# Reordering the queues of the first steps in a fused linear-attention and SoLU kernel

## The chip, the cores and the metric

The kernel runs on one core of a Trainium2 chip. The metric is the device time of one launch in microseconds (us), the median of five runs. A profile is one further execution, recorded by the hardware profiler.

## What is computed

Two blocks follow each other. The first is a recurrence over 768 positions for 4 batches x 8 heads with a 40 x 40 state each:

```
for t in range(S):
    y[t]  = rt @ state
    Sa    = state @ at
    state = state * wt - outer(Sa, bt) + outer(vt, kt)
```

The second takes y, 3072 tokens of 320 numbers, through a feed-forward block:

```
h  = x @ w_in                      # 320 -> 1024
sm = exp(h - max(h)) / (sum + 1e-9)
s  = h * sm
ln = (s - mean(s)) / sqrt(var(s) + 1e-6) * g_ln
out = ln @ w_out                   # 1024 -> 320
```

All inputs are float32 except w_in and w_out, which arrive as float64 and have to be narrowed on the chip.

## The kernel before

The recurrence is done in chunks of 64 positions. A step i treats two of the four batches of one chunk, so there are 24 steps (N); a round n is a chunk with both of its steps, 12 rounds. A step passes through several generators, each of which yields where another's work may be put between:

- `front` (from line 383) with `decay` (L345 to L374): decay factors by exponentials, the scaled k, b and a, transposes of a and b (L400, L289), and the triangular matrix nt of the chunk (pnt, L308, masked by VectorE in L311).
- `scatter` and `gather` (L424, L434, L439): the diagonal blocks of nt go to DRAM and come back with one block per partition (blk). For rounds 0 to 3 the blocks are 16 wide (`FINE`).
- `invert` or `invert_fine` (from L441): VectorE inverts the blocks column by column, a multiply and a subtract each (L456, L458). In rounds 0 to 3 one call sets up, fourteen do a column each, and a last one copies u on ScalarE (L462) and stores it by two transfers on SP (L464).
- `bring_inverse` (L499): four transfers on SP's queue bring the inverted blocks u into tinvT. Round 0 needs them for its second step only.
- `solve`: from the blocks to the inverse of the whole 64 x 64 matrix. Its first yield for i > 0 is VectorE's transposition of tinvT (L598); then py, y (L602), pz and so on (L547 for every product). For i = 0 it builds the inverse on TensorE by doubling (L584 to L593).
- `attend`: transposes of k, v and r (L289; prT is r's), the masked scores psi and lamv, and the product px.
- `recurrence` and `readout`: carry the state across chunks (px at L663, x at L665, pu at L684, nuT, lamu, sm), and give y (pyo, L723; x at L730).
- `repack` (L741 to L744, twelve transfers on SP), `hidden`, `output`: the feed-forward block, six steps (`LAG`) behind the recurrence. `store` (L812) writes a round's output by two transfers on SP.
- `weights`: fetches the 26 float64 pieces of w_in and w_out on POOL's queue (L228) and narrows them: VectorE (L179, L181), ScalarE (L184, L185), VectorE (L187, L189, L191); two calls per piece.

The order of everything is written by hand. `turns(order, ...)` reads a string; each letter advances one generator by a yield, and `I` by as many as a list of counts says. The letters: r recurrence, y readout, a attend of the next step, s solve of the next step, f and g the fronts of the step or steps five ahead, I the inverse, W the weights, B `arrivals`, X `repacked`, L a later load of b and k, * filler matmuls. Every engine and every DMA queue works its instructions off in that order.

A prologue prepares rounds 0 and 1 before step 0. Step 0 uses the second string of `EARLY` (it has two fronts), steps 1 to 5 the first. In odd steps `arrivals` brings the inverted blocks of round (i + 1) / 2 and gathers those of the round after. Step 0 ends with the scatter of round 2 and then with loads of round 3's k and round 1's r, two transfers each (L335), all on SP. A load of an input is two transfers of 64 x 16 rows of 160 bytes.

Of the kernel before, what the change touches and what calls it, by code (L numbers as in the profile page):

```python
# [19 lines left out]
L = 64  # L20
AHEAD = 5
LAG = 6
# [34 lines left out]
def doubling_masks():  # L57

    s, t = np.arange(P)[:, None] % L, np.arange(L)[None, :]
    return np.concatenate([(s // (2 * b) == t // (2 * b)) & (s & b == 0) & (t & b != 0) for b in (1, 2, 4, 8)],  # L60
                          1).astype(np.float32)
# [3 lines left out]
def kernel(  # L65
# [28 lines left out]
    nc = tc.nc  # L94
    B, H, S, D = r.shape
# [3 lines left out]
    NCH = S // L  # L99
# [176 lines left out]
    def half(p):  # L276
        return slice(64 * p, 64 * p + 64)
# [41 lines left out]
    of_round = [dict() for _ in range(NCH)]  # L319

    def load(n, *names, by=(nc.sync, nc.sync)):

        if n >= NCH:
            return
        d = of_round[n]
        for name in names:
            ap = dict(w=w, b=b, a=a, k=k, v=v, r=r)[name]
            if name in "vr":
                d[name] = dict(v=v_t, r=r_t)[name][n % 2]
                to = d[name].rearrange("q s h c -> q (s h) c")[:, :, 0:D]  # L330
            else:
                d[name] = raw.tile([P, 2, H, D], FP32, tag="raw_" + name, name="raw_" + name)
                to = d[name].rearrange("q s h c -> q (s h) c")
            for c in range(2):
                by[c].dma_start(out=to[half(c)], in_=ap[2 * c:2 * c + 2, :, n * L:(n + 1) * L, :]  # L335
                                  .rearrange("b h t d -> t (b h) d"))
# [39 lines left out]
    def quarter(q):  # L376
        return slice(Q * q, Q * q + Q)

    def homes(q, steps=slice(0, 2)):

        return slice((q * 2 + steps.start) * H, (q * 2 + steps.stop) * H)
# [36 lines left out]
    def scatter(n):  # L418

        d = of_round[n]  # L420
        d["blocks"] = dram.tile([64, Q, Q], FP32, tag="blk_dram", name="blk_dram")
        nt = d["nt"].rearrange("q s p g t -> q (s p g) t")
        for q in range(4):
            nc.sync.dma_start(out=d["blocks"][homes(q)].rearrange("h s t -> s h t"),  # L424
                              in_=nt[quarter(q), :, quarter(q % 2)])

    def gather(n):


        if n < FINE:  # L430
            R = Q // 2
            nb = of_round[n]["nb"] = two.tile([P, R, R], FP32, tag="blk", name="blk", bufs=2)
            for z in range(2):
                nc.sync.dma_start(out=nb[half(z)],  # L434
                                  in_=of_round[n]["blocks"][:, R * z:R * z + R, R * z:R * z + R])
            return
        nb = of_round[n]["nb"] = two.tile([P, Q, Q], FP32, tag="blk", name="blk", bufs=2)
        for p in range(2):
            nc.sync.dma_start(out=nb[half(p)], in_=of_round[n]["blocks"])  # L439
# [55 lines left out]
    def bring_inverse(n, steps=slice(0, 2)):  # L495

        u = of_round[n]["u"]
        for q in range(4):
            nc.sync.dma_start(  # L499
                out=ti_t[quarter(q), steps, :, :, quarter(q % 2)].rearrange("s z p g t -> s (z p g) t"),  # L500
                in_=u[homes(q, steps)].rearrange("h s t -> s h t"))
# [307 lines left out]
    def store(n):  # L809
        rows = out.rearrange("(b s) d -> s b d", b=B)[n * L:(n + 1) * L]  # L810
        for c in range(2):
            nc.sync.dma_start(out=rows[:, 2 * c:2 * c + 2, :], in_=of_round[n]["osb"][half(c)])  # L812

    def steps(part, n):
        for _ in range(n):
            if part:
                next(part, None)

    def turns(order, more, **parts):

        for x in order.split():
            n = more.get(x, 1)
            steps(parts.get(x), n.pop(0) if isinstance(n, list) else n)

    def fronts(i):

        return [j for j in ((4, 5) if i == 0 else (i + AHEAD,)) if j < N]

    EARLY = ("r r a r B W f I r r W I W s y r X W a I s f L W a I a s W f I a f W s I a f W s f W",
             "r r a r W f r r W g W s y r W a f g L W a I a s f g W a I s f g W I s a f g W I s f g W I")  # L830
    STEADY = "r b r a r B f b b o r o I o r o s y o r X I o h a f L a s a h f a I h f s h f h a f h"
    CENTRE = "r r a r f o I r o r o s y o r X I o h a f L a s a h I f s a h I f s h f s h I a f h"
    LATE = "r b r r a B b b r o o I o r o s y o r X I o h a L a s a h a I h s h h a h"
# [9 lines left out]
    def inverses():  # L843
        for n in range(1, NCH):
            yield from invert(n)

    def inverse_steps(i):

        if i == 0:
            return [5, 5, 5, 1, 0]  # L850
        if i == LAG - 1:
            return [0, 0, 4, 4, 3, 3]
        if i == LAG:
            return [3, 3, 4, 4, 4]
        if i < LAG:
            return [0, 0, 2, 2, 2, 2] if i % 2 else [3, 3, 1, 1, 0, 0]
        return [0, 7, 7] if i % 2 else [6, 7, 5]

    def warm(n, x):

        for _ in range(n):
            nc.tensor.matmul(idle[:, 0:x.shape[1]], lhsT=x[:, 0:P], rhs=x, start=True, stop=True)

    def fillers():
        while True:
            warm(1, sm_t[0].rearrange("q c g d -> q (c g d)")[:, 0:256])
            yield
# [5 lines left out]
    def arrivals(i):  # L873

        n = (i + 1) // 2
        if n < NCH:
            bring_inverse(n)
        if n + 1 < NCH:
            gather(n + 1)
        yield  # L880

    def later(n, *names):
# [3 lines left out]
    with tc.manual_schedule():  # L886
        both = (nc.sync, nc.scalar)
        load(0, "w", "b", "a", by=both)
        nc.scalar.dma_start(out=masks, in_=nc.inline_tensor(doubling_masks(), name="masks").ap())
        load(0, "k", "v")  # L890
        load(1, "w", "a", "b")
        warm(3, sm_t[0].rearrange("q c g d -> q (c g d)"))
        f, g, at, inv, so, ws = front(0), front(1), attend(0), invert(0), solve(0), weights()
        turns("f g f g f f g g f f f g g s g a", {}, f=f, g=g, s=so, a=at)
        f, g, warmer = front(2), front(3), fillers()
        scatter(0)
        load(0, "r")
        gather(0)
        load(1, "k")
        load(2, "w")  # L900
        turns("f g s f s * g a s f I s I f a s I g I s I g a I", dict(I=[2, 3, 3, 3, 3, 99]), f=f, g=g, s=so, a=at, I=inv,
              **{"*": warmer})
        load(2, "a", "b")
        bring_inverse(0, slice(1, 2))
        turns("s f W s * f a s a g s g f g W W", {}, f=f, g=g, s=so, a=at, W=ws, **{"*": warmer})
        scatter(1)
        load(2, "k")
        gather(1)
        load(1, "v")
        begin(0)  # L910
        inv = inverses()
        after, before = None, None
        for i in range(N):
            m, more, js = i - LAG, i + 1 < N, fronts(i)
            now = hidden(m) if m >= 0 else None
            parts = dict(r=recurrence(i), y=readout(i), I=inv, W=ws, h=now, b=after, o=before)
            if i == LAG:
                steps(ws, 99)
                parts["o"] = centre()
                steps(parts["o"], 1)  # L920
            parts.update(zip("fg", (front_of[j] for j in js)))
            if more:
                parts.update(a=attend(i + 1), s=solve(i + 1))
            if i % 2 == 0:
                load((i + 6) // 2, "w", "a")
                parts["L"] = later((i + 6) // 2, *("bk" if i else "b"))
            else:
                parts["X"] = repacked(i // 2)
                parts["B"] = arrivals(i)
            order = EARLY[len(js) - 1] if i < LAG else CENTRE if i == LAG else STEADY if js else LATE  # L930
            turns(order, dict(I=inverse_steps(i)), **parts)
            if i % 2:
                load((i + 3) // 2, "v", "r")
            if js and js[-1] % 2:
                scatter(js[-1] // 2)
            if i == 0:
                load(3, "k")
                load(1, "r")
            begin(i + 1)
            after, before = now, output(m) if m >= 0 else None  # L940
        for m in range(N - LAG, N):
            now = hidden(m)
            turns("b h h h h h o o h b b o o o o", {}, h=now, b=after, o=before)
            after, before = now, output(m)
        turns("b b b o o o o o o", {}, b=after, o=before)
# [30 lines left out]
```

## Time and profile before

| what | value |
|---|---|
| median of 5 runs | 677.42 us |
| the five runs | 676.04, 676.88, 677.42, 678.99, 685.69 us |
| profiled execution, its own time | 671.89 us |
| its span, first to last instruction | 669.8 us |
| mean granted TensorE clock | 0.973 |
| busy: PE, VectorE, ScalarE, POOL | 609.8, 443.2, 275.8, 119.2 us |
| pu of steps 1, 2, 3, 4, 5 on TensorE starts at | 72.69, 100.64, 121.32, 141.49, 164.12 us |

In the views, PE is TensorE and PEld its weight loads, DVE is VectorE, ACT ScalarE, POOL GpSimd, and SPq the issuing of transfers on SyncE's queue. A line of a timeline has start and length in us, engine, source line, operation, the tile written and those read, shapes, and how many instructions are merged (x4). What stands in square brackets is the idle time of the engine just before and what ended it. The time of an SPq line is that of issuing, not of the transfer.

### The profile page before, as it was taken

How to read it: one execution, taken by the hardware profiler on the slowest of the kernel's cores; microseconds unless marked ns; L12 is line 12 of the kernel's file. 1: busy time of each engine (PE TensorE's matmuls, PEld its weight loads, DVE VectorE, ACT ScalarE, POOL GpSimd, SP SyncE). 2: the span in 40 equal slices, each digit the busy share in tenths (PEclk: the TensorE clock that was granted, in tenths of full speed). 3: DMA queues.
4: the chain of work that ended last, by engine and by line, in shares of the span. 5: the costliest groups of instructions: out<-in, count | busy, mean ns of one | idle time of the engine just before them, and what ended most of it. 6: DMA issues, size and time to landing. Idle time of an engine off the chain costs nothing.

```text
span 669.8 us, 28595 instructions
## 1 busy us (share of the span) xinstructions
PE 609.8 (91%) x12579; PEld 430.4 (64%) x12579; DVE 443.2 (66%) x1203; ACT 275.8 (41%) x663; POOL 119.2 (18%) x219
## 2 busy tenths in 40 slices
PE   7787677888789999999999999999999999999996
PEld 4566566766666677667667667676765666555554
DVE  4459477584896786886876876976967844333423
ACT  3264554566335344534534443452443334412312
POOL 4424312331121121122112112211200100000000
PEclk9897779998899999999999999999999999999999
DMA  9769748485362545454453543554234020000000
GB/s 156 110 150 153 131 82 151 85 138 105 85 104 48 98 87 95 72 94 89 80 94 82 88 88 75 83 102 89 38 74 72 24 43 18 22 24 21 20 21 20
DMA packets 238155, 53.74 MB, mean 80 GB/s; under 512 B 227400, under 2 KB 235344, under 8 KB 238032
## 3 DMA queue, kind: packets, MB, share of 16 engines
q1 hardware_dynamic: 232928, 45.80, 40.1%
q0 software_dynamic: 1696, 5.25, 3.1%
q8 instruction: 99, 1.62, 1.1%
q10 hardware_dynamic: 3408, 0.87, 0.9%
q14 instruction: 24, 0.20, 0.1%
HBM read 36.95 MB, written 10.22 MB: 70 GB/s over the span
## 4 chain that ended last, share of the span: by engine, by line
PE 65%; DVE 14%; ACT 7%; issue 5%; DMA 4%; SPq 3%; ACTq 1%; DVEq 0%
PE po L799 16%; PE h L754 13%; PE pyo L723 4%; PE pz L547 3%; PE pcx L370 3%; PE plnT L794 3%; PE py L547 3%; DVE prod L486 3%; DVE u L488 2%; PE pcum L357 2%; PE plamv L308 2%; DMA raw_w<-in_w_dram 2%; DVE nmax L764 2%; PE ppsi L308 2%; PE plamu L308 2%
## 5 line engine op out<-in xcount | busy, mean ns | idle before, releaser
L754 PE MATMUL h<-w_in,xT 128*128 128x512 f32 (+1 forms) x288 | 125.0, 624 | 0.0
L799 PE MATMUL po<-w,lnT 128*128 128x320 f32 x384 | 115.9, 440 | 3.2 <-ACT lnT L795 3.2
L799 PEld LDWEIGHTS po<-w,lnT 128*128 128x128 f32 x384 | 68.3, 190 | 29.2 <-ACT lnT L795 5.8
L488 DVE TENSOR_TENSOR u<-u,prod 128x30 f32<-128x30 f32 (+7 forms) x240 | 66.6, 278 | 8.2
L486 DVE TENSOR_TENSOR prod<-blk,u 128x30 f32<-128x30 f32 (+7 forms) x240 | 65.9, 274 | 7.0
L764 DVE TENSOR_REDUCE nmax<-h 128x1 f32<-128x1024 f32 x24 | 29.3, 1222 | 52.4 <-PE h L754 52.4
L360 POOL TENSOR_TENSOR kx<-raw_b,inv 128x320 f32<-128x320 f32 x24 | 21.1, 877 | 233.5 <-ACT inv L358 214.3
L754 PEld LDWEIGHTS h<-w_in,xT 128*128 128x128 f32 (+1 forms) x288 | 38.0, 188 | 29.7 <-issue 27.7
L804 ACT ACTIVATE osb<-po,rs 128x320 f32<-128x320 f32 x24 | 12.7, 528 | 98.9 <-PE po L799 87.3
L795 ACT COPY lnT<-plnT 128x512 f32<-128x512 f32 x48 | 27.0, 587 | 41.5 <-PE plnT L794 41.4
L786 POOL TENSOR_TENSOR rs<-c,mhalf 128x1 f32<-128x1 f32 x24 | 13.2, 550 | 151.7 <-DVE c L785 150.6
L311 DVE TENSOR_TENSOR lamv<-plamv,cst 128x512 f32<-128x512 f32 x24 | 16.6, 690 | 29.9 <-PE plamv L308 29.0
L771 DVE TENSOR_TENSOR e<-h,e 128x1024 f32<-128x1024 f32 x24 | 29.4, 1224 | 10.1 <-ACT e L768 9.6
L768 ACT ACTIVATE e<-h,nmax 128x1024 f32<-128x1024 f32 x24 | 26.8, 1116 | 20.7 <-DVE nmax L764 15.3
L547 PE MATMUL py<-tinv,nt 32*32 32x32 f32 x1280 | 24.0, 196 | 12.3 <-DVE tinv L598 10.7
L633 ACT ACTIVATE tinvT<-pz 32x256 f32<-32x256 f32 x48 | 17.9, 374 | 41.0 <-PE pz L547 40.6
L370 PE MATMUL pcx<-cst,lw 128*128 128x132 f32 x192 | 32.2, 293 | 2.8 <-DVE y L602 1.5
L370 PEld LDWEIGHTS pcx<-cst,lw 128*128 128x128 f32 x192 | 26.7, 194 | 11.2 <-ACT y_mid L629 3.5
L372 ACT ACTIVATE kx<-pcx 128x264 f32<-128x264 f32 x48 | 18.9, 393 | 32.8 <-PE pcx L370 32.5
L709 POOL TENSOR_TENSOR sm<-tot,fac 128x320 f32<-128x320 f32 x20 | 14.8, 741 | 97.8 <-DVE tot L708 65.9
L776 DVE BATCH_NORM_STATS2 bs<-e 128x6 f32<-128x512 f32 x48 | 30.8, 684 | 0.6
L547 PEld LDWEIGHTS py<-tinv,nt 32*32 32x32 f32 x1280 | 20.2, 110 | 16.9 <-issue 12.7
(139 smaller groups left out, 1174.9 us busy)
## 6 DMA issues: line engine op xcount, KB each, us to landing
blk<-blk_dram SPq DMA_DIRECT2D x16, 256.0 KB
raw_k<-in_k_dram SPq DMA_DIRECT2D x24, 160.0 KB
v<-in_v_dram SPq DMA_DIRECT2D x24, 160.0 KB
r<-in_r_dram SPq DMA_DIRECT2D x24, 160.0 KB
out_dram<-osb SPq DMA_DIRECT2D x24, 160.0 KB
raw_w<-in_w_dram SPq DMA_DIRECT2D x23, 160.0 KB
raw_b<-in_b_dram SPq DMA_DIRECT2D x23, 160.0 KB
raw_a<-in_a_dram SPq DMA_DIRECT2D x23, 160.0 KB
```

Of the source, the lines that this page charges most:

```text
L308: nc.tensor.matmul(t[half(c ^ p * cross), p, g * L:(g + 1) * L], lhsT=lhs[half(p), g, half(c)], rhs=rhs[half(p), g, half(c)], start=True, ...
L370: nc.tensor.matmul(t[:, g * 132:g * 132 + 132], lhsT=pair(lw, 2 * j + g), rhs=cst[:, lo:lo + 132], start=True, stop=True)
L486: nc.vector.tensor_tensor(out=t, in0=nb[:, j:j + 1, j + 1:Q].to_broadcast([P, rows, m]), in1=u[:, 0:rows, j:j + 1].to_broadcast([P, rows, ...
L488: nc.vector.tensor_tensor(out=u[:, 0:rows, j + 1:Q], in0=u[:, 0:rows, j + 1:Q], in1=t, op=ALU.subtract)
L547: nc.tensor.matmul(t[quarter(out), c:c + Q], lhsT=lhs(p, g), rhs=rhs(p, g), start=True, stop=True)
L754: nc.tensor.matmul(h[:, j * 512:j * 512 + 512], lhsT=of_round[i // 2]["xT"][rows, kt, i % 2 * P:i % 2 * P + P], rhs=w_in[rows, 4 if kt == ...
L764: nc.vector.tensor_reduce(out=nmax, in_=h, axis=AX.X, op=ALU.max, negate=True)
L768: nc.scalar.activation(out=e, in_=h, func=AF.Exp, bias=nmax, accum_out=esum)
L771: nc.vector.tensor_tensor(out=q, in0=h, in1=e, op=ALU.mult)
L776: nc.vector.bn_stats(out=bs[:, j], in_=q[:, j * 512:j * 512 + 512])
L795: nc.scalar.copy(out=lnT[:, fs.start:fs.stop].rearrange("p f t -> p (f t)"), in_=t)
L799: nc.tensor.matmul(o[:, 0:DM], lhsT=lnT[:, f, :], rhs=w2[:, f, :], start=f == 0, stop=f == NF - 1)
```

## The change

Four things are changed, all of them orders:

- In the prologue, VectorE's inverse of round 0 is called one solve step later at its beginning and at its end. One `s` moves from the second string of turns to the first. In step 0 the first call of the inverse moves behind `a s`, with 4 yields instead of 5, and the second does 6 instead of 5.
- The loads of round 3's k and round 1's r move from the end of step 0 into `arrivals` of step 1: k between the bringing of round 1's inverted blocks and the gather of round 2, r behind that gather.
- Steps 1 to 5 no longer share a string: odd ones call the weights 11 times instead of 9, even ones 7 times.
- The second transfer of the last round's output is issued on ScalarE's queue.

```
-            nc.sync.dma_start(out=rows[:, 2 * c:2 * c + 2, :], in_=of_round[n]["osb"][half(c)])
+            (nc.scalar if c and n == NCH - 1 else nc.sync).dma_start(out=rows[:, 2 * c:2 * c + 2, :], in_=of_round[n]["osb"][half(c)])
...
-    EARLY = ("r r a r B W f I r r W I W s y r X W a I s f L W a I a s W f I a f W s I a f W s f W",
-             "r r a r W f r r W g W s y r W a f g L W a I a s f g W a I s f g W I s a f g W I s f g W I")
+    EARLY = ("r r a r B W f I r r W I W s y r X W a I s f W a W I a s W f I a W f W s I a f W s f W",
+             "r r a r W f r r W g W s y r W a f g L W a a s I f g W a I s f g W I s a f g W I s f g W I",
+             "r r a r f I r r W I W s y r X W a I s f L W a I a s f I a f W s I a f W s f W")
...
         if i == 0:
-            return [5, 5, 5, 1, 0]
+            return [4, 6, 5, 1, 0]
...
             bring_inverse(n)
+        if i == 1:
+            load(3, "k")
         if n + 1 < NCH:
             gather(n + 1)
+        if i == 1:
+            load(1, "r")
...
-        turns("f g s f s * g a s f I s I f a s I g I s I g a I", dict(I=[2, 3, 3, 3, 3, 99]), f=f, g=g, s=so, a=at, I=inv,
+        turns("f g s f s * g a s f s I f a s I g I s I I g a s I", dict(I=[2, 3, 3, 3, 3, 99]), f=f, g=g, s=so, a=at, I=inv,
...
-        turns("s f W s * f a s a g s g f g W W", {}, f=f, g=g, s=so, a=at, W=ws, **{"*": warmer})
+        turns("f W s * f a s a g s g f g W W", {}, f=f, g=g, s=so, a=at, W=ws, **{"*": warmer})
...
-            order = EARLY[len(js) - 1] if i < LAG else CENTRE if i == LAG else STEADY if js else LATE
+            order = EARLY[1 if i == 0 else 0 if i % 2 else 2] if i < LAG else CENTRE if i == LAG else STEADY if js else LATE
...
-            if i == 0:
-                load(3, "k")
-                load(1, "r")
```

## The prediction, made before the result was known

> **What bounds the kernel now.** I read the page first, in the order of its parts. From step 6 on TensorE is the bound and nothing in the change touches that stretch except the last store; the slices before it are the only ones that leave room.
>
> ```profile
> PE 609.8 (91%) x12579; PEld 430.4 (64%) x12579; DVE 443.2 (66%) x1203; ACT 275.8 (41%) x663; POOL 119.2 (18%) x219
> PE   7787677888789999999999999999999999999996
> PEclk9897779998899999999999999999999999999999
> ```
>
> A slice is 16.7 us. PE shows 6 to 8 tenths up to slice 11 (about 200 us) and 9 afterwards, so time saved before 200 us is kept, because what follows is a full TensorE queue. Then the stretches of 2 us around the emptiest place, with PE, PEld, DVE, ACT, POOL, clock, DMA share and GB/s:
>
> ```profile
> 78.00:80.00 2.00, 0.53 (x4) 0.29 (x4) 0.42 (x1) 0.59 (x1) 1.74 (x4) 1.00 0.98 182
> 80.00:82.00 2.00, 0.00 (x0) 0.00 (x0) 0.00 (x0) 0.00 (x0) 1.72 (x4) 0.61 1.19 202
> 82.00:84.00 2.00, 0.00 (x0) 0.00 (x0) 0.00 (x0) 0.00 (x0) 0.00 (x0) 0.50 1.19 161
> 84.00:86.00 2.00, 0.00 (x0) 0.00 (x0) 0.39 (x1) 0.00 (x0) 0.00 (x0) 0.50 0.50 51
> ```
>
> Every engine stands still for 6 us while the DMA engines are full, and the granted clock falls to half. The timeline of SP's queue, VectorE and TensorE says for what:
>
> ```profile
> 70.55 1.13 SPq L464 DMA_DIRECT2D u_dram<-u  x2
> 72.50 2.01 SPq L424 DMA_DIRECT2D blk_dram<-nt  x4
> 74.55 1.37 SPq L335 DMA_DIRECT2D raw_k<-in_k_dram  x2
> 75.97 1.53 SPq L335 DMA_DIRECT2D r<-in_r_dram  x2
> 78.02 4.92 SPq L499 DMA_DIRECT2D tinvT<-u_dram  x4
> 82.98 1.90 SPq L434 DMA_DIRECT2D blk<-blk_dram  x2
> ...
> 85.61 0.71 DVE L598 STREAM_TRANSPOSE tinv<-tinvT 128x512 f32<-128x512 f32 x1 [7.19 <-DMA tinvT<-u_dram]
> ...
> 86.47 1.08 PE L547 MATMUL py<-tinv,nt 32*32 32x32 f32 x64 [7.94 <-DVE tinv L598]
> ...
> 89.72 1.11 PE L289 MATMUL prT<-cst,r 128*128 128x128 f32 x4
> ```
>
> The inverted blocks of round 1 (tinvT) stand in SP's queue behind two transfers of k and two of r. VectorE waits 7.19 us for them, TensorE 7.94 us for VectorE. The last line is the one to keep in mind: 3.25 us after the wait, TensorE needs that same r.
>
> **The change, part by part.**
>
> *Prologue: VectorE's inverse of round 0 behind the solve.* No instruction is added; VectorE's order changes. (On POOL the moved steps own two zeroings of u, 0.70 us at 57.10 in step 0, and pass nothing there.) Before, three columns of the inverse (28.26 to 29.56, 1.30 us) ran in a hole in which VectorE waited for psi (30.26, idle 0.70 before it). Now two other steps (0.71 us) run there, the 1.30 us fall behind psi, and the last column (0.39 us, 36.77 to 37.16) goes behind the solve's y (37.08). So y comes 1.30 - 0.39 = 0.9 us later, and TensorE's pz at 37.47, which waited 1.20 us for y, with it. The moved step also issues two copies on ScalarE (0.83 us at 37.20) and two u transfers on SP, ahead of loads of a and b; u comes about 1.3 us later, and nobody waited for it (its transpose at 52.25 shows no idle time). Bounds: 0 if a later wait absorbs it, 1.3 if the shorter queue gains nothing. I take 0.9 us later.
>
> *Step 0: four columns behind an eviction.* VectorE ran five inverse steps (57.71 to 59.70, 2.0 us) before y at 59.70, and TensorE's pz started at 60.15 after 1.70 us of idle. With y first it is ready near 58.0, and TensorE's 1.70 us go. The number of inverse steps stays 15 up to the third call, so the last column ends at 68.26 plus the 0.9 above, near 69.2. ScalarE's copies of u (70.09, behind two bT copies that follow TensorE and now come 1.7 - 0.9 = 0.8 us earlier) can start near 69.2 to 69.3: u's store moves from 70.55 to about 69.65, the scatter from 72.50 to 71.6. Bounds for this: 0 (VectorE alone decides) to 1.7 us; taken 0.9.
>
> *SP's queue in step 1.* Four tinvT issues pass four load issues (k, k, r, r), and the two gather issues pass r. tinvT can be issued when the scatter ends, 71.6 + 2.01, so 73.7 instead of 78.02. Where nothing stood in front (123.45 to 125.40 in a later step) four such issues took 1.95 us and the last landed at 127.18, 3.7 us after the first issue. So tinvT lands at 77.4 instead of 85.48: 8.1 us earlier, and if that were all, the step would follow.
>
> But now r is last. Its transfers are issued behind tinvT, k and the gather. Best case by the shortest rows: 1.95 + 1.37 + 1.35 (gather at 125.56) + 1.53 = 6.2 us after 73.7, so 79.9, and 1.8 us more to land: 81.7. Worst case: the same ten issues took from 74.55 to 84.88 before, 10.3 us, so 84.0, and 3.3 us more (82.14 to 85.48): 87.3. I take 86.0, near the worst, because the DMA share stood at 0.98 to 1.19 from 76 to 84: the engines were full, and the order does not shorten what they carry (weights on POOL's queue, 78.26 to 80.24, included). TensorE then reaches prT near 81 and stands until 86.1 instead of 89.72. Gain 3.6 us; ends 2.4 (89.72 - 87.3) and 8.0 (89.72 - 81.7). Behind prT queue pz, plamv and all the rest of step 1. VectorE, in order, first waits for the gathered blocks (before: 87.61), which now land before r. The output blocks (xT at 86.93) find SP free at about 84 and lose nothing.
>
> *The clock.* In the rows above an idle TensorE fell to 0.50, and kept it to 90.7. At 0.50 the 32-matmul groups take 1.06 to 1.13 us, at full clock 0.69. A wait of some 5 us at prT again ends at half clock; before, only 1 us of the work after prT fell into it. Four such groups more cost 4 x 0.4 = 1.6 us, of which VectorE, ahead by what it did in the wait, leaves perhaps 1.0. Ends 0 and 1.6; taken 1.0 us.
>
> [...]
>
> *Narrowing of the weights.* Odd early steps get 11 calls instead of 9, even ones 7. Two calls narrow one piece: on VectorE 0.29 + 0.29 + 0.42 + 0.42 + 0.43 = 1.85 us in step 1 (256 wide), 0.23 + 0.23 + 0.32 + 0.32 + 0.33 = 1.43 us in later ones (160 wide), plus two ScalarE evictions and POOL's fetch. In step 1 the wait for r covers it. Step 3 has VectorE idle only 0.95, 1.11, 0.18 and 1.05 us, at waits that stay; there up to 1.4 us can show. In step 5 the weights run out, as before. Steps 2 and 4 lose a piece each, where VectorE already waited up to 1.98, 2.46, 3.92 and 3.23 us for TensorE, so little comes back. Ends: 4.7 us lost (1.85 + 1.43 + 1.43) and 2.9 gained (two pieces); taken 0.4 us lost, nearest to step 3's rows less something from step 2.
>
> *The last store.* Its two issues took 1.25 us one after the other at 665.17; ScalarE's queue issues the second beside the first. Gain 0 to 0.63, taken 0.5 us.
>
> **Sum**: -3.6 + 1.0 + 0.4 - 0.5 = -2.7 us (the first two parts are inside the 73.7). The profiled execution took 671.89 us (span 669.8 and 2.1 around it) and would take 669.2. It lies 5.5 us under the median of the runs, 677.42, which I take to stay so: 677.4 - 2.7 = 674.7 us.
>
> **The rivals.**
> - *r is no obstacle.* It lands near 82, TensorE waits about 1 us and keeps its clock: -8.0 - 0.5 + 0.4 = -8.1, so 669.3 us. For it: the short issue times at 123 us. Against: the DMA shares over 0.98.
> - *The wait only changes its name.* r lands at 87.3 and the half clock takes 1.6: -2.4 + 1.6 + 0.4 - 0.5 = -0.9, or even nothing: 676.5 us. For it: the same ten transfers, the same full engines.
> - *Slower: the narrowing shows in the odd steps.* VectorE becomes the bound there and nothing comes back in even steps: 4.7 instead of 0.4 us, so -2.7 + 4.3 = +1.6, 679.0 us. It decides once more than 3.1 us of the 4.7 show. For it: step 3 leaves VectorE 3.3 us idle at waits that the new work doesn't fill. Against: the wait for r covers step 1.
>
> **How the numbers follow.** Forecast 0.50, r no obstacle 0.15, name only 0.23, slower 0.12. Predicted: 674.7. Four of the five runs lie between 676.04 and 678.99 (the fifth at 685.69), so each case has 1.5 to 2 us about it. 8 in 10 reach from the first rival to the third: 668.5 to 679.5. One per cent is 6.8 us, about what a measurement of this kernel can tell from no change. Faster by over that (under 670.6) needs most of the first rival and a little of the forecast's tail: 0.14. Slower by over it (above 684.2) has only the tail of the third: 0.04. Within: 0.82.
>
> **What the profile will show.** Right: tinvT issued by about 74 and VectorE's transposition near 78 without 7 us of idle; in its place a TensorE wait at prT for r of some 5 us, and prT near 86; no gap before the pz at 58; pz of the prologue 0.9 us later. Wrong: prT starting before 83 with no wait (first rival), or at 88 or later (second); or VectorE gaining more than 1 us per odd step ahead of TensorE's px, with pu waiting for x (third). The prediction fails outright if u's store is later than 70.55, since then nothing in step 1 moves forward.

## The result, and the profile after

The changed kernel takes 677.57 us (median of 46 runs), the kernel before 677.38 us (86 runs). The ratio is 1.0016, 95% interval [1.0000, 1.0031]: no gain, and at most 0.3% lost. The forecast had 2.7 us gained (674.7 us); the measured time is inside its range, and inside the case "within 1%", but the forecast gain did not come. The nearest of the four cases is "the wait only changes its name" (676.5 us).

The profiled execution of the changed kernel took 677.02 us (span 675.2, mean clock 0.964), close to its median. That of the kernel before took 671.89 us, 5.5 us under its median, so the two pages can't be subtracted. Most of their difference is probably the clock: up to 210 us the records of before show 34.1 us at half clock, those of after 44.4 us. As an estimate, 10.2 us at half clock cost at most half of that, 5.1 us, if TensorE worked through all of them; the spans differ by 5.4 us. All else is therefore compared inside one trace, from one event of a step to the next.

The busy row of TensorE and the row of its granted clock, 40 slices of 16.9 us, from the page of the changed kernel:

```profile
PE   6787677897798999999999999999999999999996
PEclk9879869799999999999999999999999899999999
```

The low stretch is as long as before: 6 to 9 tenths in the first 13 slices (before, 6 to 8 in the first 12), and 9 behind them. The stretches of 2 us around the place that the change aims at (busy PE, PEld, DVE, ACT, POOL, clock, DMA share, GB/s):

```profile
80.00:82.00 2.00, 0.00 (x0) 0.00 (x0) 0.00 (x0) 0.45 (x1) 1.95 (x5) 1.00 0.85 202
82.00:84.00 2.00, 0.00 (x0) 0.00 (x0) 0.00 (x0) 0.00 (x0) 0.13 (x1) 0.87 1.11 210
84.00:86.00 2.00, 0.83 (x62) 0.86 (x64) 1.69 (x4) 0.00 (x0) 0.00 (x0) 0.50 1.02 108
88.00:90.00 2.00, 0.48 (x20) 0.29 (x12) 1.97 (x7) 0.55 (x2) 0.58 (x1) 0.50 0.71 94
```

The hole is split in two. TensorE stands still from 79.8 to 85.2 us instead of from 78.5 to 86.5, and again before 90.7; the DMA engines are nearly as full as before, and the clock is at half from 83.5 on. The timeline of SP's queue, VectorE and TensorE at the same place:

```profile
72.98 1.13 SPq L464 DMA_DIRECT2D u_dram<-u  x2
74.68 2.53 SPq L424 DMA_DIRECT2D blk_dram<-nt  x4
77.39 3.11 SPq L499 DMA_DIRECT2D tinvT<-u_dram  x4
80.55 1.59 SPq L335 DMA_DIRECT2D raw_k<-in_k_dram  x2
82.24 2.25 SPq L434 DMA_DIRECT2D blk<-blk_dram  x2
84.54 1.68 SPq L335 DMA_DIRECT2D r<-in_r_dram  x2
...
84.31 0.71 DVE L598 STREAM_TRANSPOSE tinv<-tinvT 128x512 f32<-128x512 f32 x1 [4.68 <-DMA tinvT<-u_dram]
...
85.17 1.07 PE L547 MATMUL py<-tinv,nt 32*32 32x32 f32 x64 [5.39 <-DVE tinv L598]
...
90.68 1.09 PE L289 MATMUL prT<-cst,r 128*128 128x128 f32 x4 [2.20 <-DMA r<-in_r_dram]
...
103.22 0.75 PE L684 MATMUL pu<-tinvT,x 64*64 64x64 f32 x32 [0.86 <-DVE x L665]
```

The order of SP's queue is the new one: tinvT comes right behind the scatter, and r is the last of the four. VectorE's wait shrinks from 7.19 to 4.68 us, TensorE's before py from 7.94 to 5.39 us, and a new wait of 2.20 us for r appears at prT. Measured from u's store, prT starts 17.70 us later; before it was 19.17 us (89.72 - 70.55). So 1.5 us are gained here. At pu of step 2 (103.22, 30.24 us behind u's store; before 30.09) they are gone. One pair of traces could mislead, so the same distances were read from the five kernels with the old order of this queue and the six with the new one that have no filler matmuls at this place and no early loads (the experiments below): prT stands 19.5 and 17.4 us behind u's store on the mean, pu of step 2 30.9 and 30.2 us. The gain is 2.1 us at prT, and 0.7 us of it are left at pu.

### The profile page after: what moved, and what is told of

It reads as the page before. It is cut to its first block, busy times and chain, and to the rows that moved or that the text cites. A ratio compares the mean times of both kernels' runs of the same rounds, so it can differ in the third digit from the quotient of the medians.

```text
span 675.2 us, 28596 instructions
## 1 busy us (share of the span) xinstructions
PE 614.7 (91%) x12579; PEld 435.5 (64%) x12579; DVE 444.4 (66%) x1203; ACT 276.0 (41%) x663; POOL 119.1 (18%) x219
## 3 DMA queue, kind: packets, MB, share of 16 engines
q8 instruction: 99, 1.62, 1.0%
## 4 chain that ended last, share of the span: by engine, by line
PE 69%; DVE 16%; ACT 6%; issue 5%; DMA 2%; SPq 1%; ACTq 1%; DVEq 0%
PE po L799 16%; PE h L754 13%; PE pyo L723 4%; PE pz L547 3%; PE plnT L794 3%; PE pcx L370 3%; PE py L547 3%; PE plamv L308 2%; DVE prod L486 2%; PE pcum L357 2%; DVE u L488 2%; PE plamu L308 2%; DVE nmax L764 2%; PE ppsi L308 2%; PE pvT L289 2%
## 5 line engine op out<-in xcount | busy, mean ns | idle before, releaser
L771 DVE TENSOR_TENSOR e<-h,e 128x1024 f32<-128x1024 f32 x24 | 29.4, 1224 | 10.2 <-ACT e L768 9.7
```

The source lines that it names most:

```text
L771: nc.vector.tensor_tensor(out=q, in0=h, in1=e, op=ALU.mult)
```

## The experiments

Each was run beside the kernel before on the same chip; the ratio is to that kernel, with its 95% interval. Most executions of one kernel lie within 4 us of its median, some 8 us away, so 12 runs (6 in three of the kernels) still leave about 0.35% (2.4 us) on each side, and small terms are read from the traces.

**The parts alone.** First the order of SP's queue in step 1 by itself:

```
-            if i == 0:
-                load(3, "k")
-                load(1, "r")
             begin(i + 1)
...
             bring_inverse(n)
+        if i == 1:
+            load(3, "k")
         if n + 1 < NCH:
             gather(n + 1)
+        if i == 1:
+            load(1, "r")
```

> The kernel before with only the move in SP's queue (the blocks of round 1 first, then k, the gather, r). Theory A, 'the wait changes its name': the wait for tinvT shrinks from 7.9 us to 3 to 5.5 us and a wait of 2 to 4 us for r appears at prT; prT starts about 17.7 us after u's store is issued instead of 19.2, and the half clock takes that back: the time stays within 1 us of the kernel before, 676.4 to 678.4. Theory B, the forecast on record: prT gains 3.6 us and 2.6 of them stay after the clock, so about 674.8.

Measured: 0.9986 [0.9951, 1.0022]. From u's store to prT 17.94 us (before 19.17), to pu of step 2 30.44 us (before 30.09). The part that was to bring nearly all of the gain brings 1.2 us up to prT and nothing up to pu, as in the changed kernel.

The prologue's two strings by themselves:

```
-        turns("f g s f s * g a s f I s I f a s I g I s I g a I", ...
+        turns("f g s f s * g a s f s I f a s I g I s I I g a s I", ...
-        turns("s f W s * f a s a g s g f g W W", ...
+        turns("f W s * f a s a g s g f g W W", ...
```

> The kernel before with only the two moved calls of the inverse of round 0 in the prologue. Theory A: pz of the prologue starts about 1.0 us later (38.4 instead of 37.5) and everything behind it, so the time rises by about 1 us, to 678.4. Rival: a later wait absorbs it, no change, 677.4.

Measured: 0.9988 [0.9954, 1.0022]. The prologue's last pz, for which 0.9 us was forecast, starts at 37.24 to 41.12 us in seven kernels with the new order (mean 38.9) and at 37.47 to 40.28 in eight with the old one (mean 38.8), those with fillers at the very start left out. No cost can be seen.

Step 0's order by itself:

```
-             "r r a r W f r r W g W s y r W a f g L W a I a s f g W a I s f g W I s a f g W I s f g W I")
+             "r r a r W f r r W g W s y r W a f g L W a a s I f g W a I s f g W I s a f g W I s f g W I")
...
-            return [5, 5, 5, 1, 0]
+            return [4, 6, 5, 1, 0]
```

> The kernel before with only step 0's first inverse call behind the solve step. Theory A: VectorE is the bound up to the kx products (L401), which stand behind the same nine columns in either order; y is 2 us earlier, pz up to 1 us, but kx and u's store do not move: no change, 677.4, within 0.6. Rival, the forecast on record: u's store 1.8 us earlier relative to the prologue and the time about 1 to 1.7 us shorter, 675.7 to 676.4.

Measured: 0.9997 [0.9960, 1.0034]. No gain; why is told below.

The narrowing's new strings by themselves (the three strings of `EARLY` with step 0's left as it was):

```
-            order = EARLY[len(js) - 1] if i < LAG else ...
+            order = EARLY[1 if i == 0 else 0 if i % 2 else 2] if i < LAG else ...
```

> The kernel before with only the new sharing of the narrowing, 11 calls in odd and 7 in even early steps. Theory A: nothing that can be measured, 0 to 1 us; in the trace steps 2 to 5 (from pu of step 2 to pu of step 6) take 86 to 90 us as in the other kernels. Rival (VectorE becomes the bound of the odd steps): step 3 longer than 22 us with pu waiting for x, and the time 2 us or more above the kernel before.

Measured: 1.0035 [1.0001, 1.0070], 2.4 us lost. And the reverse, the changed kernel with the one string of before for steps 1 to 5:

```
-            order = EARLY[1 if i == 0 else 0 if i % 2 else 2] if i < LAG else ...
+            order = EARLY[len(js) - 1] if i < LAG else ...
```

> The changed kernel with the narrowing shared as before, nine calls in every early step. Theory A (the new sharing costs 2 us or more, as e5_narrow's 1.0035 says, and the move in SP's queue and the store bring about as much): ratio to the kernel before 0.995 to 0.998. Rival (the sharing costs nothing in the changed kernel, where the wait for r covers it): 1.000 to 1.002, as the changed kernel.

Measured: 0.9965 [0.9930, 1.0001], against 1.0016 for the changed kernel. Both point to a cost of the narrowing, of 2.4 and 3.5 us, where 0.4 was forecast; each interval reaches nearly to none. Where it shows is the same in both kernels that have it; the changed kernel's timeline:

```profile
113.36 0.66 PE L289 MATMUL prT<-cst,r 128*128 128x128 f32 x4 [1.15 <-DVE y L602]
...
147.63 0.75 PE L684 MATMUL pu<-tinvT,x 64*64 64x64 f32 x32 [0.56 <-DVE x L665]
...
157.59 0.65 PE L289 MATMUL prT<-cst,r 128*128 128x128 f32 x4 [1.21 <-DVE y L602]
...
110.87 0.71 POOL L709 TENSOR_TENSOR sm<-tot,fac 128x320 f32<-128x320 f32 x1 [3.77 <-DVE parts L179]
112.13 0.87 POOL L360 TENSOR_TENSOR kx<-raw_k,inv 128x320 f32<-128x320 f32 x1
...
111.66 1.40 DVE L458 TENSOR_TENSOR u<-u,prod 128x14 f32<-128x14 f32 x1
112.97 0.34 DVE L602 SCALAR_TENSOR_TENSOR y<-py,cst 128x128 f32<-128x128 f32 x1
```

The same place in the kernel before:

```profile
109.79 0.66 PE L289 MATMUL prT<-cst,r 128*128 128x128 f32 x4
110.90 0.45 PE L547 MATMUL pz<-tinvT,y 32*32 32x32 f32 x30 [0.46 <-DVE y L602]
...
109.40 0.94 POOL L360 TENSOR_TENSOR kx<-raw_k,inv 128x320 f32<-128x320 f32 x1
...
109.54 0.84 DVE L456 TENSOR_TENSOR prod<-blk,u 128x14 f32<-128x14 f32 x1
```

The waits are in the even steps, 2 and 4, not in the odd ones that got the additional work. prT needs r and not y, so what it waits for is probably the PSUM buffer of py, which y reads; that is inferred from the releaser and was not tried. Before, prT of step 2 had no such wait and pz waited for y only 0.46 us. In all eight kernels with the new narrowing prT of step 2 waits 1.15 to 1.49 us; in the twelve without it, the kernel before among them, 0. At prT of step 4 the twelve wait too, 0.41 to 1.16 us, so only a part of the 1.21 is new. VectorE has a share in it: a subtraction over 14 elements takes 1.40 us instead of 0.18, over the time in which POOL works at kx. It happened before as well: in the twelve a multiplication takes 0.84 us instead of 0.15 beside the same work. In all twenty traces this operation of VectorE ends within 0.1 us of POOL's.

**Where r may stand.** If r is the new obstacle, it can be put second:

```
             bring_inverse(n)
+        if i == 1:
+            load(1, "r")
+        if i == 1:
+            load(3, "k")
         if n + 1 < NCH:
             gather(n + 1)
```

> As e1_blocks, but r of round 1 is issued directly behind the blocks, ahead of k and of the gather. Theory A (full DMA engines: what stands last lands last): r lands about 3 us earlier than in e1_blocks, the wait at prT falls from 2.8 us to 0 to 1, VectorE waits 1 to 3 us for the gathered blocks instead, and pu of step 2 starts 27 to 29 us after u's store of round 1 instead of 30.4. Rival (the wait for tinvT, not r, loses the time): still about 30 us.

Measured: 0.9992 [0.9958, 1.0027]. Its timeline of TensorE and VectorE:

```profile
87.57 0.63 PE L289 MATMUL prT<-cst,r 128*128 128x128 f32 x4 [1.86 <-DMA r<-in_r_dram]
92.12 1.08 PE L547 MATMUL pz<-tinvT,y 32*32 32x32 f32 x64 [3.92 <-issue]
...
91.04 0.29 DVE L447 TENSOR_SCALAR u<-blk 128x256 f32<-128x256 f32 x1 [6.12 <-DMA blk<-blk_dram]
```

prT now comes 14.38 us behind u's store, 4.8 us earlier than before. Then the gathered blocks are last in the queue: VectorE, in order, waits 6.12 us for them with y behind it, and pz stands 3.92 us. All of it is given back (pu 31.9 us behind u's store). Four transfers are wanted within 10 us; in both orders that were tried the one that stands last has the wait.

Or the two loads leave this place altogether: k and r are issued right behind the load of b in step 0, where SP's queue stood empty from 63.3 to 70.5 us.

```
     def later(n, *names):
         load(n, *names)
+        if n == 3:
+            load(3, "k")
+            load(1, "r")
         yield
...
-            if i == 0:
-                load(3, "k")
-                load(1, "r")
```

> The kernel before, but the four loads (k of round 3, r of round 1) stand behind the load of b in step 0, where SP's queue is idle from 63.3 to 70.5 us, so that neither stands between the scatter and the blocks nor behind the blocks. Theory A, the place of r is what gives the gain away: no wait at prT, tinvT lands 7 to 9 us after u's store is issued, VectorE waits 0 to 2 us, and the time falls by 4 to 7 us, to 670.5 to 673.5. Rival, the DMA engines are simply full or VectorE is the bound of step 1 anyway: less than 2 us, 675.5 or more.

Measured: 0.9930 [0.9895, 0.9966], the only part or rearrangement of transfers and calls that gains by itself. Its timeline:

```profile
67.28 2.30 SPq L335 DMA_DIRECT2D raw_k<-in_k_dram  x2
69.62 2.45 SPq L335 DMA_DIRECT2D r<-in_r_dram  x2
73.70 1.13 SPq L464 DMA_DIRECT2D u_dram<-u  x2
...
78.19 2.09 SPq L499 DMA_DIRECT2D tinvT<-u_dram  x4
80.45 1.36 SPq L434 DMA_DIRECT2D blk<-blk_dram  x2
...
87.44 1.11 PE L289 MATMUL prT<-cst,r 128*128 128x128 f32 x4
```

prT has no wait and stands 13.74 us behind u's store, pu of step 2 24.72 us, 5.4 us (0.8%) earlier than before. In the changed kernel the same move was tried too (its k and r in `later` in place of `arrivals`):

> The changed kernel with the four loads of k and r behind the load of b in step 0, as in e2_loads_early; all its other parts stay. Theory A (the other parts cost about 1 us in the prologue and bring nothing else but 0.5 us at the last store): 4 to 5 us below the kernel before, like e2_loads_early, ratio 0.993 to 0.995. Rival (the other parts help once the queue is free): ratio under 0.990. Second rival (they cost): 0.996 or more.

Measured: 0.9995 [0.9960, 1.0029]; prT 17.34 us and pu 29.9 us behind u's store. There tinvT, issued at 80.07, let VectorE start only at 87.25, 7.2 us later; with the loads early alone it was 5.5. POOL's four fetches of weights start 1.0 us behind tinvT's first issue there (81.08), and 3.3 us behind it with the loads early alone (81.48); in the changed kernel it is 2.1 and 6.9 us. The closer the fetches, the later VectorE's transposition starts, and not in these three alone: over the fourteen kernels that issue tinvT right behind the scatter it is 4.1 us behind tinvT's first issue where the fetches start 3.7 us behind it, 5.3 to 5.5 at 3.2 to 3.4, 5.7 to 6.9 at 2.1 to 2.9, 6.4 to 7.2 at 1.0 to 1.2. That is a correlation; an experiment without the fetches was not made. It is also only half of the story of this kernel: its tinvT is issued 6.05 us behind u's store instead of 4.49 with the loads early alone. The second transfer of u is issued 2.85 us behind the first there, 0.60 in every other kernel; the issues of r end 0.1 us ahead of it (1.6 us with the loads early alone), so the early loads just reached into the place that they were to leave.

**The clock.** If the half clock eats the gain, filler matmuls in the waits should keep it full. The changed kernel with matmuls on a buffer that nobody reads, 10 before py and 4 before prT of step 1, 256 columns each:

```
+        if i == 2:
+            warm(10, cst[:, 0:256])
         if fine:
             t = products("py16",
...
+        if i == 2:
+            warm(4, cst[:, 0:256])
         rT = d["rT"] = transposed("rT",
```

> The changed kernel with filler matmuls on TensorE in step 1, whose result nobody reads: ten of 256 columns ahead of the solve's py and four ahead of prT, so that TensorE works during most of the two waits. Theory A (the half clock behind the waits gives the gain back): the clock stays at 1.00 through the waits, prT to pu of step 2 takes 10 to 11.5 us instead of 12.5, and pu of step 2 starts about 28.5 to 29.5 us after u's store instead of 30.2. Rival (VectorE paces that stretch, the clock only fills its waits): 12 us or more, nothing gained.

Measured: 0.9904 [0.9868, 0.9940]. From prT to pu of step 2 the clock stayed full, and it took 11.34 us instead of 12.54. That alone is 1.2 us of a gain of 7, so the same count was run with 8 columns each, at both places:

```
-            warm(10, cst[:, 0:256])
+            for _ in range(10):
+                nc.tensor.matmul(idle[:, 0:8], lhsT=cst[:, 0:P], rhs=cst[:, 0:8], start=True, stop=True)
```

> As e8_fillers, with as many filler matmuls at the same two places, but of 8 columns instead of 256, so that TensorE's instruction stream is shifted by the same count while the waits stay empty. Theory A (TensorE's clock is what e8 changed): the clock falls to 0.50 in the waits as in the changed kernel and the time is that of the changed kernel, ratio to the kernel before 0.998 to 1.003. Rival (the shift of the instruction stream moved the pauses that wait for nothing shown, of up to 1.8 us, off the critical places): like e8_fillers, 0.988 to 0.993.

Measured: 0.9911 [0.9887, 0.9935], the same gain, although the clock fell to half for 20.5 us from 84.2 on, and from prT to pu it took 14.48 us. So the clock at this wait is not needed for the gain. The kernel before with 14 fillers before py, and the one with the early loads (and the last store on two queues) with 14:

> The kernel before with fourteen wide fillers (about 6.3 us of TensorE) ahead of the solve's py in step 1, in the wait of 7.9 us; SP's queue as before. Theory A: the clock stays at 1.00 through the wait, the 4 us of half clock behind it go, 1.5 to 3 us are gained there and later, ratio 0.994 to 0.998; less than e8, whose blocks also land earlier. Rival (the fillers alone are the whole of e8's gain): 0.988 to 0.992.

> A candidate: e2_loads_early with the last store on ScalarE's queue and, ahead of the solve's py in step 1, five wide fillers (2.2 us, for the 2 us wait that e2 had left) and nine of 8 columns. Theory A: the gains of the earlier loads (0.993) and of the kept clock add up, ratio 0.984 to 0.990. Rival (they are the same gain, since e2's shorter wait already keeps the clock): 0.992 to 0.994.

Measured: 0.9927 [0.9895, 0.9959] and 0.9912 [0.9884, 0.9940].

**The stream of instructions.** What all the fillers have in common is that they shift everything behind them by 28 passes (14 of these float32 matmuls in the kernel are 28 in the trace). In the traces TensorE pauses in the midst of a group, with nothing to wait for, at matmuls whose numbers lie some 127, or a multiple of it, apart: in the changed kernel at its matmul 2509, 2890, 3017, 3398 and 3654. Part 3 of the page has a queue that it calls instruction; this line is that of the changed kernel:

```profile
q8 instruction: 99, 1.62, 1.0%
```

99 packets carry 1.62 MB, 16 KB each, and 12579 matmuls by 99 are 127 to a packet (with 128 passes more there are 100): from these counts the packets are taken to go with TensorE's stream. The times of the packets in the traces tie the pauses to them: all 90 pauses of over 0.15 us in the midst of a group between 100 and 195 us, in all twenty kernels, end 1.2 to 1.9 us after a packet of this queue has ended, with a median of 1.44 us. Two of the pauses of the changed kernel:

```profile
119.91 0.37 PE L547 MATMUL py<-tinv,nt 32*32 32x32 f32 x10 [1.77 <-issue]
...
162.54 0.27 PE L308 MATMUL plamv<-rT,vT 64*64 64x64 f32 x1 [1.74 <-issue]
```

The first cuts the 32 matmuls of py after the 22nd. To tell this from a filled wait, 14 small matmuls were put at the very start, where TensorE has no work of the kernel's own until 7.8 us:

```
         warm(3, sm_t[0].rearrange("q c g d -> q (c g d)"))
+        sx = sm_t[0].rearrange("q c g d -> q (c g d)")
+        for _ in range(14):
+            nc.tensor.matmul(idle[0:32, 0:32], lhsT=sx[0:32, 0:32], rhs=sx[0:32, 0:32], start=True, stop=True)
```

> The changed kernel with 14 small matmuls (32 x 32, 28 passes) at the very start, where TensorE idles until 7.7 us; they fill nothing near step 1. If the gain of the kernels with fillers (0.990 to 0.991) comes from where TensorE's instruction stream pauses (every some 127 matmuls) and not from the waits that they were put at, this one shows it too: a ratio near 0.991, 671 us, and the mid-group pauses stand at other matmuls than in the changed kernel (which has 1.77 us at 119.91 and 1.74 at 162.54). If the gain needs fillers at the wait of step 1, the ratio stays at the changed kernel's, 1.00 to 1.003.

Measured: 0.9929 [0.9901, 0.9957]. Nothing at the waits of step 1 was touched (py waits 3.94, prT 2.87 us), and 0.9% is gained against the changed kernel. The two places in its timeline have no pause, and between 100 and 195 us one of 0.27 us is left:

```profile
116.95 0.69 PE L547 MATMUL py<-tinv,nt 32*32 32x32 f32 x32
...
155.94 0.85 PE L308 MATMUL plamv<-rT,vT 64*64 64x64 f32 x32
```

Then 64 of them, 128 passes, a whole packet:

> The same with 64 small matmuls (128 passes). If the pauses come about once in 127 to 128 matmuls, a shift by one whole period puts them back nearly where they were: a ratio near the changed kernel's, 1.00 to 1.003, with long pauses again in steps 2 and 4. If any matmul added ahead helps, or the gain has to do with a clock that the start sets, it is near 0.991 as with 14. If fillers help only at the wait, 1.00 as well, but then the kernel with 14 at the start is there too.

Measured: 1.0072 [1.0041, 1.0102]. They took 5.14 us there and put the first real matmul from 7.82 to 11.45 us; without these 3.6 us (0.53%) the ratio is 1.002, the changed kernel's own. And the pause is back at the same work, 128 matmuls further on (2637):

```profile
124.18 0.37 PE L547 MATMUL py<-tinv,nt 32*32 32x32 f32 x10 [1.77 <-issue]
```

The same 64 inside TensorE's wait for the inverted blocks, where they delay little:

> The changed kernel with 64 small matmuls (32 x 32, 128 passes) at py of step 1, where TensorE waits 5.4 us for the transposition of the inverted blocks. At the start the same 64 took 5.14 us, 3.6 of them ahead of the first real matmul; here they lie in the wait. They shift everything behind them by a whole period of the stream. Stream of instructions: the pauses come at the same work as in the changed kernel and the ratio is its own, 1.00 to 1.003. Fillers at the wait: 0.991, as with 14 of them at the same place (wide or tiny). If they don't fit into the wait, both are up to 1 us more.

Measured: 1.0005 [0.9967, 1.0043]. prT stands 18.04 us behind u's store (17.70 without them), so they cost some 0.3 us here, and 128 passes at the place where 28 gave 0.9911 give nothing. The pause is there again:

```profile
80.94 4.20 PE L603 MATMUL idle<-sm 32*32 32x32 f32 x127
...
123.35 0.37 PE L547 MATMUL py<-tinv,nt 32*32 32x32 f32 x10 [2.05 <-issue]
```

Over steps 2 to 5 (100 to 195 us) the pauses of over 0.15 us in the midst of a group add up to 2.7 to 6.5 us, mean 4.9, in the ten kernels without a shift, to 0.3 to 4.1, mean 2.2, in the eight shifted by 28 passes, and to 3.6 and 5.4 in the two shifted by 128. The stretch as a whole, from pu of step 2 to pu of step 6, takes 89.7 us on the mean in the ten, 85.4 in the eight, 90.8 and 95.6 in the two (the last in an execution 6 us over its kernel's median). So the place of the pauses is shown to matter, and it is worth more than any part of the change by itself. Of the 4.3 us in this stretch the pauses are 2.7. Time at half clock is the likely rest: from 100 to 195 us it is 14.7 us on the mean in the ten and 10.4 in the eight, with 0 to 24 us in single traces of the eight; that is only argued. What is missing to the 7 us was not taken apart.

The same shift on other orders:

> The kernel before with the same 14 small matmuls at the start. Stream of instructions: near the kernel before with fillers at py, 0.993 (0.990 to 0.996). Fillers needed at the wait: 1.000.

> The kernel before with k and r loaded behind b in step 0, the last store on two queues, and the 14 small matmuls at the start: what would be the best version if the two gains add up. The early loads alone gave 0.993, with fillers at py 0.991. Stream of instructions: 0.987 to 0.991. Fillers needed at the wait: 0.993, as the early loads alone.

> The changed kernel with the narrowing of before and the 14 small matmuls at the start. If the two gains add up (0.5 per cent from the narrowing left as it was, 0.9 from the shift of the stream), 0.988, 669 us. If a shift is worth something else with every order of VectorE, anything from 0.988 to 0.998; the kernel before with the same 14 gained only 0.4 per cent, so I lean to 0.991.

Measured: 0.9963 [0.9936, 0.9991] for the kernel before with 14 at the start, 0.9913 [0.9882, 0.9944] for the early loads with 14, 0.9958 [0.9923, 0.9992] for the changed kernel with the old narrowing and 14. The last one was 0.9965 without the shift, and the early loads 0.9930: there the shift brings nothing that can be told from noise. So the gains don't add up; what a shift is worth differs from order to order, from 0 to 1.1%. It also puts the narrowing's cost in doubt: with the shift the new narrowing (0.9929) is not slower than the old one (0.9958). The best that was found is 0.990 to 0.991, by several ways.

## Why the prediction was wrong, step by step

*The step that failed first: "u's store moves from 70.55 to about 69.65".* The text said that the prediction fails if it is later, and it is at 72.98. The 2.4 us between them stand already at prT of step 0 (57.03 instead of 54.58), with 13.7 us at half clock ahead of it instead of 3.4; that start differs from run to run (54.58 to 57.77 us over the eight kernels with the old prologue and no fillers at the start). Inside the trace, from prT of step 0 to u's store, it is 15.97 us before and 15.95 after, and over ten kernels with each order 15.93 and 15.82. What was to give 0.9 gave 0.1. y did come earlier, by about 2.0 us against prT of the same step (3.14 instead of 5.12 us behind it), and TensorE's 1.70 us are gone. But look at what follows. First the kernel before, then the changed one:

```profile
54.58 0.66 PE L289 MATMUL prT<-cst,r 128*128 128x128 f32 x4
...
64.82 1.06 PE L547 MATMUL py<-tinv,nt 32*32 32x32 f32 x32
...
59.70 0.34 DVE L602 SCALAR_TENSOR_TENSOR y<-py,cst 128x128 f32<-128x128 f32 x1
...
64.06 0.68 DVE L401 TENSOR_TENSOR kx<-paT,kx 128x512 f32<-128x512 f32 x1
```

```profile
57.03 0.66 PE L289 MATMUL prT<-cst,r 128*128 128x128 f32 x4
...
60.56 0.72 PE L370 MATMUL pcx<-cst,lw 128*128 128x132 f32 x4 [1.48 <-DVE y L602]
...
67.26 1.06 PE L547 MATMUL py<-tinv,nt 32*32 32x32 f32 x32 [1.82 <-DVE kx L401]
...
60.17 0.34 DVE L602 SCALAR_TENSOR_TENSOR y<-py,cst 128x128 f32<-128x128 f32 x1
...
66.52 1.28 DVE L401 TENSOR_TENSOR kx<-paT,kx 128x512 f32<-128x512 f32 x2
...
70.20 0.18 DVE L458 TENSOR_TENSOR u<-u,prod 128x14 f32<-128x14 f32 x1
```

VectorE does the same nine columns ahead of kx (L401) in either order, four of them before y and five behind it in the old, none before it in the new. So kx is as late as it was (9.49 us behind prT, before 9.48), and py, which now waits for kx, comes 10.23 us behind prT (before 10.24), with px, both transposes of b and, behind bT in ScalarE's order, the copies of u. Step 0's order alone was run with this as its theory, and gained nothing. The working counted the gain of TensorE at y and went on to bT as if nothing lay between; it left out kx. Its lower bound, 0 if VectorE alone decides, was the case. Even before that, pcx now waits 1.48 us for y, where it waited 0.48 us for ScalarE.

*SP's queue: gain 3.6 us (2.4 to 8.0).* Right in kind, too large: 1.5 us in the changed kernel, 1.2 us alone. The 3.6 hold the 0.9 of an earlier u's store, which did not come; counted from u's store (69.65 in the prediction), prT was to come 16.4 us behind it, with ends of 12.0 and 17.7, and it came 17.70 us behind it, at the worst end. So these bounds held; the value taken inside them, 86.0, was too early. tinvT was issued 4.4 us behind u's store instead of 7.5, as worked out (4.05). But its landing was taken as 3.7 us after the first issue, from a later step in which POOL issued one fetch of weights (125.16) and the DMA share was 0.82 from 123.45 to 127.18; here it took 6.9 (77.39 to 84.31), with POOL's five fetches at the same time and a share of up to 1.11. That the fetches are the cause is likely by the correlation above, and not shown. The DMA share of 0.98 to 1.19 that I set against r speaks against tinvT just as much, and I used it for one of the two only. r was seen as the new wait, and it came: 2.20 us at prT instead of some 5, because py ahead of it is late as well.

*The clock: 1.0 us lost (0 to 1.6).* 1.2 to 1.6: prT to pu of step 2 took 10.92 us before, with 1.0 us of it at half clock, and 12.54 after, with 6.5 us; with the queue alone it is 12.50 (6.8 us). With the clock kept full by fillers it was 11.34, so 1.2 of the 1.6 go with the clock. The term was too small because 5.5 us more ran at half clock, five groups of 1.1 us and not four. This takes back most of what the queue gained. Up to 210 us the periods at half clock in the records of the two traces are 3.4, 6.8, 10.2 and 13.7 us long. In the changed kernel the half clock from 66.4 to 73.3 us in step 0 came after 3.4 us, as long as the shortest of these periods, in which TensorE idled 2.1 us (1.15 before paT at 64.81, and 0.99 of the 1.82 before py at 67.26). In the kernel before it is alike: half clock begins at 59.98, inside the 1.70 us ahead of pz, after 3.4 us with 2.0 us idle (0.48 before pcx at 57.11, and 1.53 of the 1.70), and lasts to 73.6.

*The narrowing: 0.4 us lost (2.9 gained to 4.7).* Inside its bounds but at the bad end: 2.4 us alone (1.0035), with an interval from 0.1 to 4.7. The rival looked for it in the odd steps, and the working let the even ones only gain; the new waits are in the even ones, at prT of step 2 for y (probably by a PSUM buffer, and with VectorE slowed beside POOL). With TensorE's stream shifted the cost can't be seen, although the wait at prT is there (1.49 us), so the 2.4 us hold for this place of the pauses only.

*The prologue: 0.9 us later.* Not seen. y stands behind the inverse's columns as worked out (38.13 in the changed kernel), but pz's start varies by 3 to 4 us from kernel to kernel with either order, more than the term.

*The last store: 0.5 us.* 0.3: from its issue to the end of the span 4.31 us instead of 4.63.

Together: nothing from the first two parts, 1.5 gained and 1.6 lost by the queue and the clock, 2.4 lost in the narrowing, 0.3 gained at the end: 2.2 us slower by the terms. The measured difference is 1.1 us, from 0 to 2.1. The steps that failed are thus the 0.9 us at u's store (0.1), the rest of the queue's term (2.7 forecast, 1.5 measured), the clock's (1.0, up to 1.6) and the narrowing's (0.4, some 2.4). That the time came out inside the range owes something to luck, since the place of TensorE's pauses in the midst of a group, which the prediction did not know of, moves it by up to 1.1%.

What the prediction did well: r was seen as the new wait, the worst end of the queue's term was the measured one, and "changes its name" was named with 0.23. It should have had the largest chance. The step from a wait to its successor was worked out for one successor; in step 0 and in step 1 there was another right behind. One reading of the rows was too wide: not every engine stands still for 6 us; POOL is busy for 1.72 us of 80 to 82, and all stand still only from 81.9 to 85.6.

## What to carry to other kernels

When a wait ends on one of several transfers wanted within a short time, look first at whether their order only decides who waits, as it did here; the gain came from moving two transfers to where their queue was empty, and it did not show in the kernel in which they reached into the next store. When an operation is moved ahead on an in-order engine, ask which later operation of the same engine still has the same work in front of it: that one, and not the moved one, sets the end. And when a kernel's rearrangements are compared within 1%, shift TensorE's stream by some matmuls in an idle place as a control: that alone was worth 0 to 1.1% here.

## What the runs showed of the hardware that was not expected

- TensorE pauses in the midst of a group with nothing to wait for, 1.77 us at 119.91 in the changed kernel and 2.05 us at 123.35 with the 64 matmuls at py. Over steps 2 to 5 the pauses of over 0.15 us add up to 4.9 us on the mean in the kernels without a shift, each ends 1.2 to 1.9 us after a packet of the queue of part 3 (99 packets of 16 KB, one to 127 matmuls), and moving them by 28 passes changed the time by 0 to 1.1%.
- 64 small matmuls (32 x 32) at the start took 5.14 us, and 14 of them 1.07 us: 0.04 us a pass. They did not hold the clock: with the 64 it fell to half at 9.18 us, after 3.4 us in which TensorE was never idle, and with the 64 at py at 86.05 us, again after 3.4 us without idle time.
- A VectorE operation of 0.18 us took 1.40 us, and ended within 0.1 us of the end of POOL's multiplication at its side (113.00); in the twelve kernels with the old narrowing one of 0.15 us took 0.84 us at the same work of POOL's.
- The four transfers of tinvT, which landed 3.7 us after the first issue at a mean DMA share of 0.82 and beside one fetch of weights, took 4.1 to 7.2 us in step 1 of the fourteen kernels that issue them right behind the scatter, the longer the closer the fetches of weights stood behind them.
